# A power of two and its inverse in one masked two-column step of VectorE, and a power of two for z's factor

## The chip, the cores and the metric

One core of a Trainium2 chip runs the kernel. The metric is device microseconds from launch to end of that core, the median of several runs. The kernel before took 486.66 us (three runs, 485.74 to 486.75). TensorE is called PE here, VectorE DVE, ScalarE ACT, GpSimd POOL and SyncE SP, as in the profile.

## The reference

```python
# q, k, v: (8 batches, 8 heads, 576 rows, 64), float32
k_p, v_p = k.reshape(B,H,72,8,D).mean(3), v.reshape(B,H,72,8,D).mean(3)
scores = (q @ k_p.T) / 8;  scores -= scores.max(-1)
attn = exp(scores);  attn /= attn.sum(-1) + 1e-9
x = (attn @ v_p) as (4608 tokens, 512)
h = x @ w_in                                   # (4608, 1024)
e = exp(h - h.max(-1));  sm = e / (e.sum(-1) + 1e-9)
solu = h * sm
ln = (solu - mean(solu)) / sqrt(var(solu) + 1e-6) * g_ln
out = ln @ w_out                               # (4608, 512)
```

q and k are drawn 8 times wider than v. w_in, w_out and g_ln come as float64, so the kernel takes float32 words out of pairs of integers first.

## The kernel before, in words

All matrix products run on PE in float16 with two terms per operand: a high part (the scaled value rounded to float16) and a low part (what the rounding left). To scale without losing bits, q, pooled k, pooled v, w_in, w_out and g_ln each get a power of two just above their largest value, `p`, and its inverse, `s`. `p` comes from a maximum by keeping the exponent bits alone (`exp_bits`, line 276, an integer AND and OR on a 128x1 tile); `s` is its reciprocal in another DVE instruction. For q both are in `q_scale` (line 455: scaled maximum at 461, bits at 467, reciprocal at 472), for k and v in `a_unit` (line 494: bits through line 277, reciprocal at 499), for the weights in `w_bound`, `wi_scale`, `g_all` and `wo_scale` (lines 699 to 766).

The 4608 tokens are 36 tiles of 128. For each tile: q is scaled and split (`q_hi` on ACT, `q_lo` on DVE, line 866), turned, and multiplied with kT into `scores`; DVE and ACT make the softmax (`s_max`, `s_sub`, `s_exp`, `e_sum`, `e_rec`, `e_mul`); POOL makes its low part (`e_lo`, line 978); PE multiplies with v (`av`) and then w_in (`mm1`, tile `hp`). `h_max` and `h_nb` give the bias of the exponential; `z_scale` (line 1056) makes the factor of solu from it in three DVE steps: magnitude of `nb` (1059), reciprocal (1064), minimum with 1 and a per-batch factor (1066). Any factor per row would do, since the normalisation that follows divides it out; `n_u` on POOL puts it into the 1e-6. `z_mul` (line 1073) forms solu, ACT centres and splits it, POOL makes its low part (`z_lo`, line 1093), and `mm2` multiplies with w_out.

The weights are unpacked at the start: DVE joins the words (`w_tail`, line 657), POOL multiplies the sign in (`w_mul`, line 678: 128x1024 in one instruction), and ACT and PE split them. k and v of each later batch are pooled on POOL (line 400).

The order of all this is written out by hand: the table `ORDER` gives every operation a rank, and operations are issued by rank, so each engine runs its own in that order and a late one holds up all that stand behind it on its engine. DMAs and DMA transposes are issued on SP's queue.

Of the kernel before, what the change touches and what calls it, by code (L numbers as in the profile page):

```python
# [10 lines left out]
F32 = mybir.dt.float32  # L11
# [5 lines left out]

EXPMASK = 0x7F800000
S14 = float(2**14)
DEC = 2.0**-111  # L20
# [9 lines left out]
        "a_par.v": (129, 236, 483, 786, 1025, 1171, 1479, 1802),  # L30
        "a_unit.k": (39, 57, 211, 213, 451, 455, 657, 663, 882, 890, 1129, 1155, 1390, 1437, 1615,
        1616),
        "a_unit.v": (131, 134, 254, 261, 500, 503, 804, 805, 1027, 1029, 1180, 1181, 1481, 1482,
        1804, 1805),
        "av": (215, 257, 276, 333, 383, 463, 506, 573, 561, 661, 775, 702, 842, 893, 952, 977,
# [101 lines left out]
        1383, 1444, 1662, 1676, 1722),  # L137
        "q_scale": (30, 31, 32, 183, 189, 190, 231, 232, 247, 436, 443, 446, 666, 670, 671, 718,
        748, 750, 947, 964, 969, 1124, 1127, 1128, 1215, 1216, 1217, 1446, 1447, 1448, 1675, 1677,
        1678, 1723, 1725, 1727),  # L140
        "r_hi": (135, 262, 504, 811, 1085, 1195, 1484, 1806),
# [78 lines left out]
        1883, 1926, 1990, 1980, 2050, 2024),  # L220
        "z_scale": (267, 279, 280, 314, 322, 323, 366, 368, 371, 431, 450, 458, 462, 501, 510,
# [6 lines left out]
        "z_var": (361, 359, 440, 514, 569, 570, 637, 736, 731, 809, 887, 899, 960, 1033, 1104,  # L228
# [6 lines left out]
def kernel(  # L235
# [10 lines left out]
    nc = tc.nc  # L246
# [65 lines left out]
    nc.scalar.activation(ident16, ident, AF.Copy)  # L312
    nc.vector.tensor_scalar(out=identb, in0=ident, scalar1=1.0 / S14, scalar2=None, op0=ALU.mult)
    nc.gpsimd.memset(pmat4, 1.0)
# [13 lines left out]
    nc.gpsimd.memset(phalf, -0.5)  # L328
    for n, c in enumerate((2.0**-11, -(2.0**-11), 2.0**-7)):
        nc.gpsimd.memset(c3[:, n : n + 1], c)  # L330
# [115 lines left out]
    def q_abs(key, part):  # L446
# [6 lines left out]
        )  # L453

    def q_scale(key, n):
        if n == 0:
            st = grp["q", key] = {}
            for x in ("p", "s"):
                st[x] = sm.tile([P, 1], F32, tag=x + "q", name=f"{x}q{key}")
            a = amx["m" if key[0] == "m" else "q"]  # L460
            nc.vector.tensor_scalar(
                out=st["p"], in0=a[:, :1], scalar1=a[:, (1 if key[0] == "b" else 0) :][:, :1],
                scalar2=1.0 / S14, op0=ALU.max, op1=ALU.mult,
            )
# [809 lines left out]
    def group_q(key, t):  # L1274
# [141 lines left out]
    def tile(i):  # L1416
# [56 lines left out]
        op("act", 1.4, t(0, 6.6), h_exp, i, r=[("h", i)] + K("nb") + hk, w=K("z", "se"))  # L1473
        for n in range(2):
            op("dve", 0.2, t(0, 6.7 + 0.2 * n), z_scale, i, n, r=K("nb", "pz") if n else K("nb"),
               w=K("pz"))
        op("dve", 0.21, t(0, 7.3), z_scale, i, 2, r=K("pz") + hk, w=K("rs"))
        op("dve", 1.36, t(0, 7.5), z_mul, i, r=[("h", i)] + K("z", "rs"), w=K("z", "sz"))
# [71 lines left out]
```

## Time and profile before

| | before |
|---|---|
| median of three runs | 486.66 us |
| span of the profiled execution, first to last instruction | 483.6 us |
| PE busy | 456.5 us (94%) |
| DVE busy | 372.2 us (77%), 787 instructions |
| ACT busy | 335.2 us (69%) |
| POOL busy | 304.5 us (63%) |

The profiled execution has no launch around it: its 483.6 us stand against 486.66 us of the median run, so about 3.1 us lie outside the span. The profile lists each instruction's start and length by the source line that made it, what ended a wait before it, and the chain of work that ended last, followed back from the last instruction.

### The profile page before, as it was taken

The numbers are of one execution on the slowest core, as the hardware profiler recorded it, in microseconds if no ns is written. First come the engines' busy times: TensorE is split into PE (matmuls) and PEld (weight loads), VectorE is DVE, ScalarE is ACT, GpSimd is POOL, SyncE is SP. The second block draws the span as 40 slices with busy tenths as digits, with TensorE's granted clock in tenths as the row PEclk, the third lists the DMA queues.
The fourth block names the chain that finished last, engine by engine and source line by source line (L and its number), as shares of the span: only waits on it lengthen the run. The fifth ranks groups of instructions, "written<-read, shape, count | busy, mean of one in ns | idle before, by whom it ended". The sixth has DMA issues, their size and how long they took to land.

```text
span 483.6 us, 14740 instructions
## 1 busy us (share of the span) xinstructions
PE 456.5 (94%) x5976; PEld 287.7 (59%) x5976; DVE 372.2 (77%) x787; ACT 335.2 (69%) x557; POOL 304.5 (63%) x525
## 2 busy tenths in 40 slices
PE   1779899999999999999999999999999999999996
PEld 1655455655655556555556667666776666755553
DVE  5988999999889789878798867678878887462320
ACT  5598887677966688796677657587585697456361
POOL 3459737696697985858953597717758625643532
PEclk9989999999999999999999999999999999999999
DMA  8999389998999899999994999689899576861742
GB/s 309 395 354 225 86 114 219 196 193 138 213 237 213 209 173 207 204 229 229 161 215 111 215 245 172 126 136 243 167 229 190 115 137 117 138 142 24 153 108 69
DMA packets 197749, 88.92 MB, mean 184 GB/s; under 512 B 174121, under 2 KB 182321, under 8 KB 197169
## 3 DMA queue, kind: packets, MB, share of 16 engines
q1 hardware_dynamic: 197680, 87.98, 85.9%
q8 instruction: 47, 0.77, 0.6%
q14 instruction: 22, 0.17, 0.1%
HBM read 36.70 MB, written 9.44 MB: 95 GB/s over the span
## 4 chain that ended last, share of the span: by engine, by line
PE 78%; DVE 16%; DMA 2%; issue 2%; ACT 1%; SPq 0%; POOL 0%; ACTq 0%; DVEq 0%
PE op L274 35%; PE hp L274 31%; PE xp L999 4%; PE sc L274 3%; DMA kr<-in_k_dram 2%; DVE q L866 2%; DVE m L1041 1%; PE krps L410 1%; DVE sc L934 1%; DVE mx L920 1%; DVE sc L923 1%; DVE z L1073 1%; DVE e L949 1%; PE vrps L410 1%; PE res_wi L810 1%
## 5 line engine op out<-in xcount | busy, mean ns | idle before, releaser
L274 PE MATMUL hp<-wi,xT 128*64 128x512 f16 x1728 | 197.2, 379 | 2.8 <-DVE z L1073 1.4
L274 PE MATMUL op<-wo,zT 128*64 128x512 f16 x1728 | 197.2, 379 | 0.1
L274 PEld LDWEIGHTS <-xT 128*64 128x64 f16 x1728 | 106.6, 110 | 75.2 <-ACT xT L1008 2.0
L274 PEld LDWEIGHTS <-zT 128*64 128x64 f16 x1728 | 106.5, 110 | 70.6 <-DMA zT<-z 0.5
L1093 POOL TENSOR_TENSOR z<-z,z 128x512 f16<-128x512 f32 x71 | 82.0, 1167 | 67.9 <-ACT z L1087 66.4
L978 POOL TENSOR_TENSOR e<-e,e 128x512 f16<-128x512 f32 x36 | 42.2, 1173 | 39.7 <-ACT e L972 39.6
L1041 DVE TENSOR_REDUCE m<-hp 128x1 f32<-128x1024 f32 x36 | 43.8, 1217 | 23.1 <-PE hp L274 22.9
L1082 ACT ACTIVATE z<-z,sz 128x1024 f32<-128x1024 f32 x36 | 41.2, 1143 | 17.4 <-DVE z L1073 17.4
L1073 DVE SCALAR_TENSOR_TENSOR z<-hp,rs,z 128x1024 f32<-128x1024 f32 x36 | 46.1, 1280 | 9.1 <-ACT z L1052 7.9
L1052 ACT ACTIVATE z<-hp,nb,Hb 128x1024 f32<-128x1024 f32 x32 | 38.3, 1196 | 11.7 <-DVE nb L1044 9.1
L1151 ACT ACTIVATE osb<-op,f 128x512 f32<-128x512 f32 x36 | 24.5, 679 | 31.3 <-PE op L274 8.1
L1087 ACT ACTIVATE z<-z 128x1024 f16<-128x1024 f32 x36 | 37.7, 1050 | 0.9 <-DMA zT<-z 0.4
L1106 ACT ACTIVATE junk<-z 128x1024 f16<-128x1024 f32 x36 | 37.7, 1048 | 0.3
L400 POOL TENSOR_TENSOR vr<-vr 128x512 f32<-128x512 f32 (+3 forms) x42 | 36.9, 888 | 0.6
L400 POOL TENSOR_TENSOR kr<-kr 128x512 f32<-128x512 f32 (+3 forms) x42 | 36.7, 882 | 1.0 <-DMA kr<-in_k_dram 0.2
L920 DVE TENSOR_REDUCE mx<-sc 128x8 f32<-128x576 f32 x36 | 27.0, 750 | 12.9 <-PE sc L274 12.6
L934 DVE TENSOR_REDUCE sc<-sc 128x8 f32<-128x576 f32 x36 | 27.3, 759 | 12.2 <-ACT sc L930 12.1
L999 PEld LDWEIGHTS <-vb 128*64 128x64 f16 x960 | 28.9, 111 | 6.7 <-DVE vb L574 1.0
L1012 DVE SCALAR_TENSOR_TENSOR xT<-xp,xT 128x512 f16<-128x512 f32 x36 | 24.5, 681 | 8.9 <-ACT xT L1008 8.8
L999 PE MATMUL xp<-eT,vb 128*64 128x128 f16 (+1 forms) x960 | 31.0, 215 | 0.3 <-ACT e L975 0.3
L274 PEld LDWEIGHTS <-qT 128*64 128x64 f16 x1152 | 24.7, 114 | 9.9 <-ACT dg_wi L803 3.4
L1008 ACT ACTIVATE xT<-xp 128x512 f16<-128x512 f32 x36 | 21.2, 589 | 12.2 <-PE xp L999 12.2
(237 smaller groups left out, 621.3 us busy)
## 6 DMA issues: line engine op xcount, KB each, us to landing
kr<-in_k_dram SPq DMA_DIRECT2D x16, 512.0 KB
qr<-in_q_dram SPq DMA_DIRECT2D x16, 512.0 KB
vr<-in_v_dram SPq DMA_DIRECT2D x16, 512.0 KB
out_dram<-osb SPq DMA_DIRECT2D x32, 256.0 KB
wor<-in_moe_w_out_dram SPq DMA_DIRECT2D x4, 1024.0 KB
wo<-in_moe_w_in_dram SPq DMA_DIRECT2D x2, 1024.0 KB
wir<-in_moe_w_in_dram SPq DMA_DIRECT2D x2, 1024.0 KB
zT<-z SPq DMA_TRANSPOSE x72
```

Source lines behind the costliest of these rows:

```text
L274: nc.tensor.matmul(out[lo : lo + 64] if m > 64 else out, lhsT=lhsT[:, lo : lo + 64], **kw)
L400: nc.gpsimd.tensor_tensor(out=dst, in0=src[:, :, :n], in1=src[:, :, n : 2 * n], op=ALU.add)
L934: nc.vector.tensor_reduce(out=tl[i]["r0"], in_=s_view(i), axis=AX.X, op=ALU.add)
L978: nc.gpsimd.tensor_tensor(out=e_main(i, 1), in0=e_src(i)[0], in1=e_main(i, 0), op=ALU.subtract)
L999: nc.tensor.matmul(xp[64 * e : 64 * e + 64, c, lo:hi], lhsT=vb[b % 2][:, n, c, e], rhs=eT[:, 2 * c + e if n < 2 else H + e, lo:hi], start= ...
L1041: nc.vector.tensor_reduce(out=small(i, "m"), in_=tl[i]["hp"], axis=AX.XY, op=ALU.max)
L1052: nc.scalar.activation(z, t["hp"], AF.Exp, bias=t["nb"], scale=hsc(i, 0), accum_out=small(i, "se"))
L1073: nc.vector.scalar_tensor_tensor(out=t["z"], in0=t["hp"], scalar=t["rs"], in1=t["z"], op0=ALU.mult, op1=ALU.mult, accum_out=small(i, "sz"),)
L1082: nc.scalar.activation(t["zf"], t["zf"], AF.Identity, bias=t["sz"], scale=-float(DFF))
L1087: nc.scalar.activation(t["z16"][:, 0], t["zf"], AF.Copy)
L1093: eng.tensor_tensor(out=t["z16"][:, 1, fs], in0=t["zf"][:, fs], in1=t["z16"][:, 0, fs], op=ALU.subtract)
L1106: nc.scalar.activation(junk, t["zf"], AF.Square, scale=DFF**-0.5, accum_out=small(i, "V"))
```

## The change

One helper, `unit`, takes the place of `exp_bits` and the reciprocals. A new constant tile `flip` holds 0 and 2^127 in two columns. One `scalar_tensor_tensor` reads the maximum broadcast to two columns, masks it to the even part of the exponent (`EVENMASK`), and XORs it with `flip`: the first column is then a power of two (at most four times smaller than the maximum's), the second its inverse. The scales around it are moved by the factors 2 and 4 that this leaves. q, k, v, w_in, g_ln and w_out use it. For z, two steps remain of three: the exponent of `nb` is masked and inverted in one integer step, and the minimum follows where the reciprocal stood.

```diff
-    def exp_bits(dst, src):
-        nc.vector.tensor_scalar(
-            out=dst.bitcast(I32), in0=src.bitcast(I32), scalar1=EXPMASK, scalar2=1 << 23,
-            op0=ALU.bitwise_and, op1=ALU.bitwise_or,
+    def unit(dst, src):
+        nc.vector.scalar_tensor_tensor(
+            out=dst.bitcast(I32), in0=src.bitcast(I32).to_broadcast([P, 2]), scalar=EVENMASK,
+            in1=flip.bitcast(I32), op0=ALU.bitwise_and, op1=ALU.bitwise_xor,
         )
...
-    pw1 = const.tile([P, 1], F32, name="pw1")
+    flip = const.tile([P, 2], F32, name="flip")
...
+    for n, c in enumerate((0.0, 2.0**127)):
+        nc.gpsimd.memset(flip[:, n : n + 1], c)
...
+    def pair(key, nm, x):
+        t = sm.tile([P, 2], F32, tag="ps" + nm, name=f"ps{nm}{key}")
+        grp[nm, key].update(p=t[:, :1], s=t[:, 1:])
+        unit(t, x)
...
-        elif n == 1:
-            p = grp["q", key]["p"].bitcast(I32)
-            nc.vector.tensor_scalar(
-                out=p, in0=p, scalar1=EXPMASK, scalar2=1 << 23, op0=ALU.bitwise_and,
-                op1=ALU.bitwise_or,
-            )
-        else:
-            nc.vector.reciprocal(out=grp["q", key]["s"], in_=grp["q", key]["p"])
+        else:
+            pair(key, "q", grp["q", key]["x"])
...
-    def a_unit(nm, key, n):
-        st = grp[nm, key]
-        if n == 0:
-            exp_bits(st["p"], st["p"])
-        else:
-            nc.vector.reciprocal(out=st["s"], in_=st["p"])
+    def a_unit(nm, key):
+        pair(key, nm, grp[nm, key]["x"])
...
+    def w_unit(nm, gm):
+        t = const.tile([P, 2], F32, name=f"ps_{nm}")
+        unit(t, gm)
+        return t[:, :1], t[:, 1:]
...
     def wi_scale():
-        w_bound("wi", 1.0 / S14)
-        sw = const.tile([P, 1], F32, name="sw_wi")
-        nc.vector.reciprocal(out=sw, in_=wst["wi"]["gm"])
-        wst["wi"]["s"] = sw
+        wst["wi"]["p"], wst["wi"]["s"] = w_bound("wi", 2.0 / S14)
...
-        w_bound("wo", 2.0**-13)
+        wst["wo"]["p"], sw = w_bound("wo", 2.0**-11)
         sg = const.tile([P, CO], F32, name="sg_wo")
-        nc.vector.tensor_tensor(
-            out=pw1, in0=wst["wo"]["gm"], in1=wst["gm"], op=ALU.mult
-        )
-        sw = const.tile([P, 1], F32, name="sw_wo")
-        nc.vector.reciprocal(out=sw, in_=pw1)
         nc.vector.tensor_scalar(
-            out=sg, in0=g_sb, scalar1=sw, scalar2=None, op0=ALU.mult
+            out=sg, in0=g_sb, scalar1=sw, scalar2=wst["gs"], op0=ALU.mult, op1=ALU.mult
         )
...
             nc.vector.tensor_scalar(
-                out=small(i, "pz"), in0=t["nb"], scalar1=-1.0, scalar2=t["nb"], op0=ALU.mult,
-                op1=ALU.max,
-            )
-        elif n == 1:
-            nc.vector.reciprocal(out=t["pz"], in_=t["pz"])
+                out=small(i, "pz").bitcast(I32), in0=t["nb"].bitcast(I32), scalar1=EXPMASK,
+                scalar2=EXPMASK, op0=ALU.bitwise_and, op1=ALU.bitwise_xor,
+            )
...
-                out=small(i, "rs"), in0=t["pz"], scalar1=1.0, scalar2=hsc(i, 2), op0=ALU.min,
+                out=small(i, "rs"), in0=t["pz"], scalar1=4.0, scalar2=hsc(i, 2), op0=ALU.min,
...
-        "a_unit.v": (131, 134, 254, 261, 500, 503, 804, 805, 1027, 1029, 1180, 1181, 1481, 1482,
-        1804, 1805),
+        "a_unit.v": (131, 254, 500, 804, 1027, 1180, 1481, 1804),
```

On PE, ACT and SP the order of instructions is the same before and after. POOL has two more memsets at the start. DVE's rows in the program go from 751 to 683. Three places on DVE follow.

The scale of q's first batch, on DVE in the first 21 us. `amx_q` and `amx_k` are the maxima of q and pooled k, `pq`/`sq` the power and its inverse, which are the two columns of `psq` afterwards. Before:

```order
L461 TENSOR_SCALAR pq('b', 0)_205<-amx_q 128x1
L467 TENSOR_SCALAR pq('b', 0)_205<-pq('b', 0)_205 128x1
L472 RECIPROCAL sq('b', 0)_206<-pq('b', 0)_205 128x1
L430 TENSOR_REDUCE amx_k<-kp_87 128x1
L492 TENSOR_REDUCE pk_215<-gk_212 128x1
```

And after:

```order
L462 TENSOR_SCALAR xq('b', 0)_207<-amx_q 128x1
L273 SCALAR_TENSOR_TENSOR psq('b', 0)_209<-xq('b', 0)_207,flip 128x2
L428 TENSOR_REDUCE amx_k<-kp_87 128x1
L486 TENSOR_REDUCE xk_216<-gk_213 128x1
L852 SCALAR_TENSOR_TENSOR q_0_218<-qr_184,psq('b', 0)_209,q_0_218 128x8x64
```

Two instructions with one tensor input each have become one that reads two tensors of SBUF, and the maximum of k stands right behind it.

The scale of w_in, on DVE about 26 us in. `gm_wi` is its bound, `sw_wi` the inverse, `ct` the scale of the scores, `kT` the low part of k that the first scores need. Before:

```order
L499 RECIPROCAL sk_216<-pk_215 128x1
L657 SCALAR_TENSOR_TENSOR wor_288<-wor_288,u_wo_290 128x1024
L690 TENSOR_REDUCE gm_wi<-g_wi 128x1
L701 TENSOR_SCALAR gm_wi<-gm_wi 128x1
L277 TENSOR_SCALAR gm_wi<-gm_wi 128x1
L709 RECIPROCAL sw_wi<-gm_wi 128x1
L561 TENSOR_SCALAR ct('b', 0)_317<-pq('b', 0)_205,pk_215 128x1
L536 SCALAR_TENSOR_TENSOR kT_300<-kTp_230,sk_216,kT_300 128x576
```

And after:

```order
L647 SCALAR_TENSOR_TENSOR wor_289<-wor_289,u_wo_291 128x1024
L680 TENSOR_REDUCE gm_wi<-g_wi 128x1
L691 TENSOR_SCALAR gm_wi<-gm_wi 128x1
L273 SCALAR_TENSOR_TENSOR ps_wi<-gm_wi,flip 128x2
L551 TENSOR_SCALAR ct('b', 0)_316<-psq('b', 0)_209,psk_221 128x1
L526 SCALAR_TENSOR_TENSOR kT_300<-kTp_231,psk_221,kT_300 128x576
```

The reciprocals of k and of w_in are gone, and the new two-input step stands between the join of a w_out word (`wor`), whose end lets POOL multiply its sign, and `kT`.

The factor of z of the first tile, on DVE about 66 us in. Before:

```order
L1044 TENSOR_SCALAR nb_943<-m_891,Hb_860 128x1
L944 RECIPROCAL r_948<-sc_765 128x8
L1059 TENSOR_SCALAR pz_950<-nb_943 128x1
L1012 SCALAR_TENSOR_TENSOR xT_918<-xp_893,xT_918 128x512
L949 TENSOR_TENSOR e_953<-sc_765,r_948 128x576
L866 SCALAR_TENSOR_TENSOR q_5_937<-qr_709,sq('b', 1)_838,q_5_937 128x8x64
L1064 RECIPROCAL pz_950<-pz_950 128x1
L1066 TENSOR_SCALAR rs_994<-pz_950,Hb_860 128x1
L1073 SCALAR_TENSOR_TENSOR z_945,sz_996<-hp_803,rs_994,z_945 128x1024
```

And after:

```order
L1045 TENSOR_SCALAR pz_942<-nb_935 128x1
L998 SCALAR_TENSOR_TENSOR xT_911<-xp_886,xT_911 128x512
L935 TENSOR_TENSOR e_945<-sc_759,r_940 128x576
L852 SCALAR_TENSOR_TENSOR q_5_930<-qr_703,psq('b', 1)_833,q_5_930 128x8x64
L1050 TENSOR_SCALAR rs_985<-pz_942,Hb_854 128x1
L1057 SCALAR_TENSOR_TENSOR z_937,sz_987<-hp_797,rs_985,z_937 128x1024
```

The reciprocal is gone and `rs` stands in its place; both steps left read one tensor.

## Rows read from the trace of the kernel before

**Rows 1.** Stretches: length; busy PE, PEld, DVE, ACT, POOL; granted clock; DMA share, GB/s.

```profile
0.00:120.00 120.00, 96.98 (x1264) 61.94 (x1266) 108.07 (x228) 90.47 (x146) 73.87 (x111) 0.99 0.90 222
120.00:460.00 340.00, 339.95 (x4536) 215.65 (x4534) 261.21 (x553) 235.88 (x399) 223.88 (x398) 1.00 0.89 177
```

**Rows 2.** The chain that ended last, 0 to 125 us: start, us, what.

```profile
26.79 0.74 DVE kT L536
27.67 1.17 PE sc L274 x32
...
115.89 1.22 DVE z L1073 x2
117.15 5.37 PE hp L274 x48
```

**Rows 3.** Waits of PE: what waited for whom, us in total, times, longest.

```profile
PE sc L274 <- DVE kT L536: 3.2, 1, 3.2
```

**Rows 4.** Timeline of DVE, 18 to 27 us: start, length, instruction.

```profile
18.95 0.15 DVE L467 TENSOR_SCALAR pq('b', 0)_205<-pq('b', 0)_205 128x1 int32<-128x1 int32 x1
19.36 0.49 DVE L430 TENSOR_REDUCE amx_k<-kp 128x1 bf16<-128x320 f32 x1
...
24.56 0.16 DVE L499 RECIPROCAL sk<-pk 128x1 f32<-128x1 f32 x1
...
26.33 0.15 DVE L277 TENSOR_SCALAR gm_wi<-gm_wi 128x1 int32<-128x1 int32 x1
26.52 0.16 DVE L709 RECIPROCAL sw_wi<-gm_wi 128x1 f32<-128x1 f32 x1
26.60 0.20 DVE L561 TENSOR_SCALAR ct('b', 0)_317<-pq('b', 0)_205,pk 128x1 f32<-128x1 f32 x1
26.71 0.81 DVE L536 SCALAR_TENSOR_TENSOR kT<-kTp,sk,kT 128x576 f16<-128x576 f32 x1
```

**Rows 5.** Timeline of POOL, 17 to 31 us.

```profile
17.92 2.12 POOL L678 TENSOR_TENSOR wo<-wo,sg_wi 128x1024 f32<-128x1024 f32 x1
26.04 2.14 POOL L678 TENSOR_TENSOR wor<-wor,sg_wo 128x1024 f32<-128x1024 f32 x1 [6.00 <-DVE wor L657]
28.14 2.16 POOL L678 TENSOR_TENSOR wir<-wir,sg_wi 128x1024 f32<-128x1024 f32 x1
```

**Rows 6.** Timeline of DVE, two instructions that read two SBUF tensors.

```profile
46.61 2.17 DVE L866 SCALAR_TENSOR_TENSOR q<-qr,sq('b', 0)_206,q 128x512 f16<-128x512 f32 x1
...
177.47 0.74 DVE L591 SCALAR_TENSOR_TENSOR vr<-vp,sv,vr 64x64 f16<-64x64 f32 x1
```

**Rows 7.** Timeline of POOL at the same places.

```profile
45.80 1.19 POOL L400 TENSOR_TENSOR kp<-kr 128x128 f32<-128x128 f32 x3
46.95 2.43 POOL L400 TENSOR_TENSOR vr<-vr 128x512 f32<-128x512 f32 x2
...
176.98 1.16 POOL L978 TENSOR_TENSOR e<-e,e 128x512 f16<-128x512 f32 x1
```

**Rows 8.** Lines 591 and 866 alone: ns of one, least/median/most, first and last start.

```profile
L591 DVE SCALAR_TENSOR_TENSOR vr<-vp,sv,vr x8: 271/278/970, 45.7 to 395.5; 64x64 f16<-64x64 f32 x8
L866 DVE SCALAR_TENSOR_TENSOR q<-qr,sq('b', 1)_838,q x4: 741/742/752, 67.6 to 88.3; 128x512 f16<-128x512 f32 x4
```

**Rows 9.** Groups of DVE instructions by shape: busy us, mean ns of one, idle before.

```profile
L760 DVE TENSOR_TENSOR pw<-gm_wo,gm_g 128x1 f32<-128x1 f32 x1 | 0.2, 159 | 0.0
```

**Rows 10.** Timeline of DVE, 64 to 104 us: the bits of v's and k's power.

```profile
64.58 0.15 DVE L277 TENSOR_SCALAR pv<-pv 128x1 int32<-128x1 int32 x1
...
103.38 0.15 DVE L277 TENSOR_SCALAR pk<-pk 128x1 int32<-128x1 int32 x1
```

**Rows 11.** Timeline of POOL at the same places.

```profile
63.93 2.13 POOL L678 TENSOR_TENSOR wor<-wor,sg_wo 128x1024 f32<-128x1024 f32 x1 [3.45 <-ACT sg_wo L675]
...
102.67 1.16 POOL L978 TENSOR_TENSOR e<-e,e 128x512 f16<-128x512 f32 x1
```

**Rows 12.** A stretch, PE alone: length, busy, granted clock, DMA share, GB/s.

```profile
27.00:30.50 3.50, 2.83 (x42) 0.52 1.05 404
```

More of the change, by code (lines that the diff above doesn't have):

```diff
@@ L18 @@
 EXPMASK = 0x7F800000
+EVENMASK = 0x7F000000
 S14 = float(2**14)
@@ L30 @@
         "a_par.v": (129, 236, 483, 786, 1025, 1171, 1479, 1802),
-        "a_unit.k": (39, 57, 211, 213, 451, 455, 657, 663, 882, 890, 1129, 1155, 1390, 1437, 1615,
-        1616),
-        "a_unit.v": (131, 134, 254, 261, 500, 503, 804, 805, 1027, 1029, 1180, 1181, 1481, 1482,
-        1804, 1805),
+        "a_unit.k": (39, 211, 451, 657, 882, 1129, 1390, 1615),
+        "a_unit.v": (131, 254, 500, 804, 1027, 1180, 1481, 1804),
         "av": (215, 257, 276, 333, 383, 463, 506, 573, 561, 661, 775, 702, 842, 893, 952, 977,
@@ L137 @@
         1383, 1444, 1662, 1676, 1722),
-        "q_scale": (30, 31, 32, 183, 189, 190, 231, 232, 247, 436, 443, 446, 666, 670, 671, 718,
-        748, 750, 947, 964, 969, 1124, 1127, 1128, 1215, 1216, 1217, 1446, 1447, 1448, 1675, 1677,
-        1678, 1723, 1725, 1727),
+        "q_scale": (30, 31, 183, 189, 231, 232, 436, 443, 666, 670, 718, 748, 947, 964, 1124,
+        1127, 1215, 1216, 1446, 1447, 1675, 1677, 1723, 1725),
         "r_hi": (135, 262, 504, 811, 1085, 1195, 1484, 1806),
@@ L220 @@
         1883, 1926, 1990, 1980, 2050, 2024),
-        "z_scale": (267, 279, 280, 314, 322, 323, 366, 368, 371, 431, 450, 458, 462, 501, 510,
[6 rows of a table removed]
+        "z_scale": (267, 279, 314, 322, 366, 368, 431, 450, 462, 501, 527, 529, 588, 610, 624,
[4 rows of a table added]
         "z_var": (361, 359, 440, 514, 569, 570, 637, 736, 731, 809, 887, 899, 960, 1033, 1104,
@@ L312 @@
     nc.scalar.activation(ident16, ident, AF.Copy)
-    nc.vector.tensor_scalar(out=identb, in0=ident, scalar1=1.0 / S14, scalar2=None, op0=ALU.mult)
+    nc.vector.tensor_scalar(out=identb, in0=ident, scalar1=2.0 / S14, scalar2=None, op0=ALU.mult)
     nc.gpsimd.memset(pmat4, 1.0)
@@ L328 @@
     nc.gpsimd.memset(phalf, -0.5)
-    for n, c in enumerate((2.0**-11, -(2.0**-11), 2.0**-7)):
+    for n, c in enumerate((0.0, 2.0**127)):
+        nc.gpsimd.memset(flip[:, n : n + 1], c)
+    for n, c in enumerate((2.0**-11, -(2.0**-11), 2.0**-9)):
         nc.gpsimd.memset(c3[:, n : n + 1], c)
@@ L453, in q_abs @@
         )
+    def pair(key, nm, x):
+        t = sm.tile([P, 2], F32, tag="ps" + nm, name=f"ps{nm}{key}")
+        grp[nm, key].update(p=t[:, :1], s=t[:, 1:])
+        unit(t, x)
     def q_scale(key, n):
         if n == 0:
-            st = grp["q", key] = {}
-            for x in ("p", "s"):
-                st[x] = sm.tile([P, 1], F32, tag=x + "q", name=f"{x}q{key}")
+            st = grp["q", key] = {"x": sm.tile([P, 1], F32, tag="xq", name=f"xq{key}")}
             a = amx["m" if key[0] == "m" else "q"]
             nc.vector.tensor_scalar(
-                out=st["p"], in0=a[:, :1], scalar1=a[:, (1 if key[0] == "b" else 0) :][:, :1],
-                scalar2=1.0 / S14, op0=ALU.max, op1=ALU.mult,
-            )
-        elif n == 1:
-            p = grp["q", key]["p"].bitcast(I32)
-            nc.vector.tensor_scalar(
-                out=p, in0=p, scalar1=EXPMASK, scalar2=1 << 23, op0=ALU.bitwise_and,
-                op1=ALU.bitwise_or,
+                out=st["x"], in0=a[:, :1], scalar1=a[:, (1 if key[0] == "b" else 0) :][:, :1],
+                scalar2=2.0 / S14, op0=ALU.max, op1=ALU.mult,
             )
         else:
-            nc.vector.reciprocal(out=grp["q", key]["s"], in_=grp["q", key]["p"])
+            pair(key, "q", grp["q", key]["x"])
     def spread(src, n, name):
@@ L489, in a_all @@
         st = grp[nm, key]
-        for x in ("p", "s"):
-            st[x] = sm.tile([P, 1], F32, tag=x + nm, name=f"{x}{nm}{key}")
-        nc.vector.tensor_reduce(out=st["p"], in_=st["g"], axis=AX.XY, op=ALU.max)
-    def a_unit(nm, key, n):
-        st = grp[nm, key]
-        if n == 0:
-            exp_bits(st["p"], st["p"])
-        else:
-            nc.vector.reciprocal(out=st["s"], in_=st["p"])
+        st["x"] = sm.tile([P, 1], F32, tag="x" + nm, name=f"x{nm}{key}")
+        nc.vector.tensor_reduce(out=st["x"], in_=st["g"], axis=AX.XY, op=ALU.max)
+    def a_unit(nm, key):
+        pair(key, nm, grp[nm, key]["x"])
     def k_tile(b):
@@ L703, in w_bound @@
         )
-        exp_bits(gm, gm)
+        return w_unit(nm, gm)
+    def w_unit(nm, gm):
+        t = const.tile([P, 2], F32, name=f"ps_{nm}")
+        unit(t, gm)
+        return t[:, :1], t[:, 1:]
     def wi_scale():
-        w_bound("wi", 1.0 / S14)
-        sw = const.tile([P, 1], F32, name="sw_wi")
-        nc.vector.reciprocal(out=sw, in_=wst["wi"]["gm"])
-        wst["wi"]["s"] = sw
+        wst["wi"]["p"], wst["wi"]["s"] = w_bound("wi", 2.0 / S14)
     def w_pwi():
         nc.gpsimd.tensor_scalar(
-            out=pw3, in0=c3, scalar1=wst["wi"]["gm"], scalar2=None, op0=ALU.mult
+            out=pw3, in0=c3, scalar1=wst["wi"]["p"], scalar2=None, op0=ALU.mult
         )
@@ L771, in w_pwo @@
         nc.gpsimd.tensor_scalar(
-            out=pwo, in0=pw1, scalar1=-(2.0**-8), scalar2=None, op0=ALU.mult
+            out=pwo, in0=wst["wo"]["p"], scalar1=wst["gp"], scalar2=-(2.0**-8), op0=ALU.mult,
+            op1=ALU.mult,
         )
@@ L1113, in n_u @@
         nc.gpsimd.tensor_scalar(
-            out=u, in0=t["pz"], scalar1=1.0, scalar2=None, op0=ALU.min
+            out=u, in0=t["pz"], scalar1=4.0, scalar2=0.25, op0=ALU.min, op1=ALU.mult
         )
@@ L1212, in scale @@
                 w=[("p" + nm, key), ("s" + nm, key)])
-        for j in range(2):
-            n_ = op("dve", 0.16, t + 0.7 + 0.2 * j, a_unit, nm, key, j, u=[("p" + nm, key)],
-                    w=[("s" + nm, key)], after=[n_])
+        op("dve", 0.16, t + 0.7, a_unit, nm, key, u=[("p" + nm, key)], w=[("s" + nm, key)],
+           after=[n_])
     def pool(b, nm, t):
@@ L1283, in group_q @@
         prev = None
-        for j in range(3):
+        for j in range(2):
             prev = op("dve", 0.18, t + 2.2 + 0.2 * j, q_scale, key, j,
-                      r=[] if j else [("am", "q", key)], u=[("sq", key)] if j == 2 else [],
-                      w=[("pq", key), ("sq", key)] if j < 2 else [("sq", key)], after=[prev])
+                      r=[] if j else [("am", "q", key)], w=[("pq", key), ("sq", key)],
+                      after=[prev])
             if j == 0:
@@ L1473, in tile @@
         op("act", 1.4, t(0, 6.6), h_exp, i, r=[("h", i)] + K("nb") + hk, w=K("z", "se"))
[L1474 to L1477, printed above, removed]
+        op("dve", 0.2, t(0, 6.7), z_scale, i, 0, r=K("nb"), w=K("pz"))
+        op("dve", 0.21, t(0, 7.3), z_scale, i, 1, r=K("pz") + hk, w=K("rs"))
         op("dve", 1.36, t(0, 7.5), z_mul, i, r=[("h", i)] + K("z", "rs"), w=K("z", "sz"))
```

4 lines of the change are left out of this document (1 added, 3 removed), and 10 rows, old and new, of the table ORDER.

## The prediction, made before the changed kernel ran

> **What bounds the kernel now.** I read the stretches first, then the chain of waits, then the waits of PE, then the timelines of DVE and POOL side by side. The stretches split the kernel in two [rows 1]: from 120 to 460 us PE is busy for 339.95 of 340.00 us, so nothing that DVE saves there can shorten it; before 120 us PE is busy for 96.98 us and DVE for 108.07. Whatever the change is worth is decided in the first 120 us, by when PE gets its work. The chain shows the hand-over [rows 2]: `z_mul` of a tile ends at 117.11 us, PE goes on at 117.15 us, and from there it is PE to the end. Its first step on this side of the loads is `kT` at 26.79, then the first scores at 27.67 us, for which PE had stood 3.2 us [rows 3]. In between PE and DVE pass the delay to and fro, so a step of DVE that comes later there makes the end later, and one that comes earlier makes it earlier.
>
> **The change part by part.** It removes one instruction of DVE for each power of two (q, k, v, w_in, g_ln), two for w_out and one per tile for z. A removed step is worth between 0.08 us, where the next is independent (26.52 to 26.60), and 0.19 us, where it sits in a chain (26.33 to 26.52) [rows 4]. The z step that stays reads one tensor as before: 0.
>
> What it adds is a new kind of instruction: the step that makes both numbers reads two tensors in SBUF. Its own length is not in the trace; the nearest rows are 159 ns for a two-input step of one column [rows 9] and 278 ns for one of 64 columns [rows 8]. I take 0.16 us, the same as what it replaces.
>
> The cost is elsewhere. Two-input steps of DVE are stretched when POOL is in the middle of an instruction. The one of 64 columns took 0.74 us at 177.47 [rows 6] instead of 0.28 [rows 8], beside a POOL instruction from 176.98 to 178.14 [rows 7]: it must have begun at 177.93, 0.2 us before POOL's row ended. The q step at 46.61 took 2.17 us instead of 0.74, so it began at 48.04, about 0.2 us before the first of two POOL instructions of 1.2 us from 46.95 ended [rows 6 to 8]. So I price a unit step that meets a running POOL instruction as: it starts when that row ends, less 0.2 us, and all of DVE behind it waits.
>
> [...]
>
> Now the places, in the times of before.
> - q's first batch. The unit step is due at 18.95; POOL multiplies signs from 17.92 to 20.04 [rows 4, 5]. It starts at 19.84, and `amx_k`, which stood at 19.36, follows at about 19.95: +0.6 us. Behind it wait PE's spread of k's maximum and the whole of DVE's queue.
> - w_in. Without k's reciprocal at 24.56 DVE is 0.1 us better, so +0.5. POOL's next sign instruction (26.04 to 28.18) is released by DVE itself [rows 5], so it moves to 26.54 to 28.68. The unit step comes to 26.83 and is let in at 28.48. `ct` and `kT` follow in 0.24 us: `kT` starts at 28.72 instead of 26.71, +2.0 us, and the first scores with it.
> - From 28 to 48 us everything behind moves by these 2.0 us, POOL's work too, since it hangs on the same softmax. The unit steps of g, v and w_out lie here, and two removed steps of w_out; but the q step at 46.61 waits 1.43 us for POOL in any case [rows 6, 7], so what is lost here up to that, and all that is gained, is swallowed: 0.
> - From 48 to 117 us twelve steps go: five of z, three of q, two of k, two of v. At 0.08 to 0.19 us that is 1.0 to 2.3 us; most stand between independent steps, so I take 0.1 each: -1.2 us.
> - v of the second batch. The step due at 64.58 meets the last sign instruction (63.93 to 66.06) [rows 10, 11]; it starts at 65.86: +1.3 us.
> - k of the third batch. Due at 103.38 within 102.67 to 103.83 [rows 10, 11]: it starts at 103.63, +0.25 us. The other unit steps between 48 and 117 us I put at 0.
>
> The sum is 2.0 + 0 - 1.2 + 1.3 + 0.25 = +2.35 us. The profiled span of 483.6 us becomes 486.0 us; the median of the runs lies 3.1 us above the span, so 486.66 becomes 489.0 us. After 120 us the waits come too, but PE has no gap there that they could open at once.
>
> [...]
>
> **The rivals.**
> 1. Faster: the new step is not held up. It reads two columns only, and no row of before shows a two-input step in the middle of a sign instruction of 2.1 us. Then `amx_k` gains nothing (it waits for pooled k), `kT` gains 0.1 for k's reciprocal and 0.19 for w_in's, 28 to 48 us is swallowed, and 1.2 us come after: -1.5 us, 485.2 us. Against it stands the 64-column step [rows 6 to 8], whose own work is hardly longer. It decides if the unit step of w_in is under 0.3 us long in the new trace. [...]
> 2. A missed turn: POOL's sign instructions stand back to back (28.14 starts before 26.04 + 2.14 ends [rows 5]). The q step at 46.61 was not let in where POOL's short ones changed over at 46.99 [rows 6, 7]. If w_in's step misses the change at 28.18, it waits for 2.1 us more: 491.1 us. For it that row, against it that long instructions let DVE in at 48.04.
> 3. No change: the 2.0 us vanish in PE's later stops. PE is idle for 23 us of the first 120 [rows 1], some of it after 28 us. Then only the later terms count, +0.35 us: 487.0 us. Against it: those stops are waits for DVE, which is held up itself.
>
> **How the numbers follow.** The forecast has 0.60, rival 1 0.13, rival 2 0.14, rival 3 0.13. The forecast's own range is 487.7 to 490.3 us: a removed step at 0.19 instead of 0.1 gives 1.1 us back, a missed small turn or a longer unit step of 0.28 us (eleven of them, 0.12 each) costs up to 1.3. The range to hold eight in ten reaches down to 486.0 and up to 491.4 us; below lies most of rival 1. A change of 0.2%, 1.0 us, is what can be told from none here. Faster by more: most of rival 1, 0.11. Within: rival 3 and the rest, 0.16. Slower: 0.73.
>
> **What would show it.** In the new profile, the unit steps (line 273) should be of two kinds: 0.16 us where POOL is idle, and 0.9 us for q's first batch, 1.6 us for w_in, 1.3 us for v's second batch, each ending with a POOL instruction of the sign line. PE's wait for `kT` should be about 5.2 us. If all unit steps are short, rival 1 is right; if PE's wait is longer but PE stands busy from before 120 us as now, rival 3; if w_in's step is near 3.7 us, rival 2. I am wrong altogether if the time moves through anything after 120 us.

## The result: slower by more than twice the forecast

The changed kernel took 492.75 us (median of five runs, 491.19 to 494.73) against 486.75 us of the kernel before (485.74 to 487.06). The ratio is 1.0121, interval 1.0099 to 1.0143: 6.0 us slower where 2.3 us were forecast, and outside the range. The execution whose profile is shown was the longest of the five (494.73 us, span 493.0; the other four spans are 489.5 to 491.5), so a difference between the two traces can be larger than that of the medians: the profiled spans, 493.0 and 483.6 us, are 9.4 us apart.

The stretches answer [rows 1] and [rows 12]; the columns are the same.

```profile
0.00:120.00 120.00, 94.65 (x1164) 60.35 (x1166) 105.86 (x196) 86.61 (x136) 71.74 (x105) 0.94 0.86 214
120.00:460.00 340.00, 337.31 (x4550) 224.31 (x4548) 258.90 (x512) 237.15 (x404) 224.26 (x396) 1.00 0.87 175
25.30:35.30 10.00, 5.51 (x46) 2.72 (x46) 8.51 (x12) 7.88 (x9) 5.28 (x4) 0.50 0.98 307
49.10:52.40 3.30, 3.30 (x23) 1.35 (x23) 3.17 (x7) 2.40 (x5) 3.21 (x6) 0.50 0.15 50
```

DVE is busy 2.2 us less before 120 us, but PE too, by 2.3 us: what DVE saves, PE doesn't get. After 120 us PE now stands for 2.7 of 340 us, where it stood for 0.05. The granted clock was 0.50 in two stretches, of 10 and 3.3 us; before, it was 0.52 in one of 3.5.

The waits of PE (whom it waited for, us in all, times, longest). The first was 3.2 us before [rows 3], the second 0.8.

```profile
PE sc L270 <- DVE kT L526: 4.7, 1, 4.7
PE g_wo L270 <- DVE g_wo L676: 2.6, 1, 2.6
...
PE gv L270 <- DVE amx_v L428: 1.4, 2, 1.0
```

The chain that ended last, to 125 us, answers [rows 2]. Four unit steps (line 273) now stand on it.

```profile
18.74 1.20 DVE psq('b', 0)_209 L273
...
26.94 1.85 DVE ps_wi L273
28.91 0.73 DVE kT L526
29.79 1.17 PE sc L270 x32
...
45.23 2.14 DVE psv L273
...
68.75 1.41 DVE psv L273
```

The first scores start at 29.79 instead of 27.67 us. Here are DVE, then POOL, around the first two held steps; they answer [rows 4] and [rows 5].

```profile
18.74 1.20 DVE L273 SCALAR_TENSOR_TENSOR psq('b', 0)_209<-xq('b', 0)_207,flip 128x2 int32<-128x2 int32 x1
19.94 0.49 DVE L428 TENSOR_REDUCE amx_k<-kp 128x1 bf16<-128x320 f32 x1
...
21.64 0.15 DVE L273 SCALAR_TENSOR_TENSOR psk<-xk,flip 128x2 int32<-128x2 int32 x1
...
26.94 1.85 DVE L273 SCALAR_TENSOR_TENSOR ps_wi<-gm_wi,flip 128x2 int32<-128x2 int32 x1
28.72 0.20 DVE L551 TENSOR_SCALAR ct('b', 0)_316<-psq('b', 0)_209,psk 128x1 f32<-128x1 f32 x1
28.84 0.80 DVE L526 SCALAR_TENSOR_TENSOR kT<-kTp,psk,kT 128x576 f16<-128x576 f32 x1
```

```profile
17.80 2.12 POOL L668 TENSOR_TENSOR wo<-wo,sg_wi 128x1024 f32<-128x1024 f32 x1
26.66 2.12 POOL L668 TENSOR_TENSOR wor<-wor,sg_wo 128x1024 f32<-128x1024 f32 x1 [6.73 <-DVE wor L647]
28.73 2.14 POOL L668 TENSOR_TENSOR wir<-wir,sg_wi 128x1024 f32<-128x1024 f32 x1
```

With POOL idle the step takes 0.15 us (21.64). The one at 18.74 ends at 19.94, POOL's product at 19.92; the one at 26.94 ends at 28.79, POOL's at 28.78. That is the mechanism and the size of the forecast. Next, DVE and then POOL at v of the first batch and the q step of [rows 6] and [rows 7].

```profile
45.23 2.14 DVE L273 SCALAR_TENSOR_TENSOR psv<-xv,flip 128x2 int32<-128x2 int32 x1
47.29 0.41 DVE L676 TENSOR_REDUCE g_wo<-bnd_wo 128x1 f32<-128x256 f32 x1
...
52.30 0.74 DVE L852 SCALAR_TENSOR_TENSOR q<-qr,psq('b', 0)_209,q 128x512 f16<-128x512 f32 x1
```

```profile
44.00 2.13 POOL L668 TENSOR_TENSOR wor<-wor,sg_wo 128x1024 f32<-128x1024 f32 x1
46.09 3.16 POOL L398 TENSOR_TENSOR kr<-kr 128x512 f32<-128x512 f32 x4
49.22 1.14 POOL L398 TENSOR_TENSOR kp<-kr 128x128 f32<-128x128 f32 x3
50.31 2.07 POOL L398 TENSOR_TENSOR vr<-vr 128x512 f32<-128x512 f32 x2
```

The step of v came at 45.23, wasn't let in where POOL changed over at 46.1, and ended only at 47.37, among the four sums that followed. The maximum of w_out's bound (`g_wo`) stood behind it, and PE waited for that. The q step that took 2.17 us before takes 0.74 here: moved by 5.7 us, it comes just as one of POOL's sums ends (52.38). So there was nothing to swallow the loss.

Here are DVE and POOL at v of the second batch, answering [rows 10] and [rows 11].

```profile
68.66 1.50 DVE L273 SCALAR_TENSOR_TENSOR psv<-xv,flip 128x2 int32<-128x2 int32 x1
```

```profile
68.01 2.13 POOL L668 TENSOR_TENSOR wor<-wor,sg_wo 128x1024 f32<-128x1024 f32 x1 [2.28 <-ACT sg_wo L665]
```

It ends at 70.16, POOL's product at 70.14. Last, DVE, POOL and PE around 250 us, where before PE had no gap.

```profile
249.92 0.66 DVE L273 SCALAR_TENSOR_TENSOR psq('m', 2)_4611<-xq('m', 2)_4604,flip 128x2 int32<-128x2 int32 x1
250.50 2.13 DVE L273 SCALAR_TENSOR_TENSOR psk<-xk,flip 128x2 int32<-128x2 int32 x1
252.56 1.21 DVE L1027 TENSOR_REDUCE m<-hp 128x1 f32<-128x1024 f32 x1
```

```profile
250.48 0.30 POOL L967 TENSOR_TENSOR e<-e,e 128x64 f16<-128x64 f32 x1
250.74 0.45 POOL L398 TENSOR_TENSOR vp<-vr 128x128 f32<-128x128 f32 x1
251.15 1.15 POOL L964 TENSOR_TENSOR e<-e,e 128x512 f16<-128x512 f32 x1
252.27 0.30 POOL L967 TENSOR_TENSOR e<-e,e 128x64 f16<-128x64 f32 x1
```

```profile
259.29 0.25 PE L270 MATMUL gv<-identb,amx_v 128*64 128x128 bf16 x2 [0.99 <-DVE amx_v L428]
...
260.53 0.86 PE L985 MATMUL xp<-eT,vb 128*64 128x128 f16 x24 [0.47 <-DVE pz L1045]
```

Two unit steps one after the other hold DVE up for 2.7 us, through changes of POOL at 250.74, 251.15 and 252.27. The row maximum (line 1027) and all behind it are late, and the batch's next maximum, `amx_v`, misses PE by 0.99 us. In the trace of before that maximum ended at 249.51 us and PE took it up at 250.54, so the margin, 1.0 us, could be read there:

```profile
249.02 0.49 DVE L430 TENSOR_REDUCE amx_v<-vp 128x1 bf16<-128x320 f32 x1
250.54 0.22 PE L274 MATMUL gv<-identb,amx_v 128*64 128x128 bf16 x2
```

### The profile page after: what moved, and what is told of

Read it like the earlier page. It is cut to its first block, busy times and chain, and to the rows that moved or that the text cites. A ratio compares the mean times of both kernels' runs of the same rounds, so it can differ in the third digit from the quotient of the medians.

```text
span 493.0 us, 14666 instructions
## 1 busy us (share of the span) xinstructions
PE 461.0 (94%) x5976; PEld 303.2 (62%) x5976; DVE 371.3 (75%) x719; ACT 336.1 (68%) x557; POOL 306.5 (62%) x527
## 4 chain that ended last, share of the span: by engine, by line
PE 76%; DVE 14%; DMA 6%; issue 2%; ACT 2%; SPq 1%; POOL 0%; ACTq 0%; DVEq 0%
PE op L270 33%; PE hp L270 29%; PE xp L985 4%; PE sc L270 3%; DMA qr<-in_q_dram 3%; PE res_wi L796 2%; DMA eT<-e 2%; DMA qT<-q 1%; DVE q L852 1%; DVE z L1057 1%; PE vrps L408 1%; DVE m L1027 1%; DVE mx L906 1%; DVE psv L273 1%; DVE amx_q L440 1%
## 5 line engine op out<-in xcount | busy, mean ns | idle before, releaser
L270 PEld LDWEIGHTS <-xT 128*64 128x64 f16 x1728 | 112.5, 110 | 67.7 <-ACT xT L994 1.5
L270 PEld LDWEIGHTS <-zT 128*64 128x64 f16 x1728 | 114.2, 110 | 64.3 <-DMA zT<-z 1.2
L270 PE MATMUL sc<-kT,qT 128*64 128x72 f16 x1152 | 26.1, 200 | 5.8 <-DVE kT L526 4.7
```

What stands on the lines that cost most here:

```text
L270: nc.tensor.matmul(out[lo : lo + 64] if m > 64 else out, lhsT=lhsT[:, lo : lo + 64], **kw)
```

## The experiments

Each ratio is to the kernel before, run on the same chip beside it.

**Two one-input steps.** The changed kernel, with the unit step cut in two:

```diff
-        nc.vector.scalar_tensor_tensor(
-            out=dst.bitcast(I32), in0=src.bitcast(I32).to_broadcast([P, 2]), scalar=EVENMASK,
-            in1=flip.bitcast(I32), op0=ALU.bitwise_and, op1=ALU.bitwise_xor,
-        )
+        for n in range(2):
+            nc.vector.tensor_scalar(
+                out=dst[:, n : n + 1].bitcast(I32), in0=src.bitcast(I32), scalar1=EVENMASK,
+                scalar2=n * EVENMASK, op0=ALU.bitwise_and, op1=ALU.bitwise_xor,
+            )
```

> The changed kernel, but the power and its inverse come from two steps of one tensor input each (mask; mask and XOR) in place of the one step that reads two tensors of SBUF. The z part and the order stay. Blocked reads (the two-input step waits for POOL): no step of line 273 and 274 is over 0.3 us, PE's wait for kT is 3.0 us or less, and the time is 485.2 us, 0.3% under before. Shifted order (the steps that are gone move other work of DVE and SP into worse places): the time stays near that of the changed kernel, 491 to 493 us, since the order is the same. Clock alone: as blocked reads, since without the longer stop of PE its clock does not fall longer.

Measured: 483.36 us, ratio 0.993 (0.9913 to 0.9947), faster than both kernels, and 1.8 us under what I expected. The two steps of w_in, beside the same POOL product (26.38 to 28.52):

```profile
26.67 0.21 DVE L274 TENSOR_SCALAR ps_wi<-gm_wi 128x1 int32<-128x1 int32 x2
26.80 0.20 DVE L552 TENSOR_SCALAR ct('b', 0)_319<-psq('b', 0)_209,psk 128x1 f32<-128x1 f32 x1
26.92 0.81 DVE L527 SCALAR_TENSOR_TENSOR kT<-kTp,psk,kT 128x576 f16<-128x576 f32 x1
```

Together they take 0.21 us instead of 1.85. The new arithmetic is harmless; the form of the step is not.

**The two halves of the change.** z's part alone on the kernel before (its `z_scale` of two steps, and the factor 4 that goes with it), and the unit steps alone (z's three steps put back):

> The kernel before with the z part of the change alone (two z steps of three). Blocked reads: both z steps read one tensor, so nothing waits; up to five reciprocals of 0.1 to 0.19 us are gone before PE is saturated, 0 to 0.7 us faster: 486.0 to 486.7 us. Shifted order: slower by a good part of the 6 us, since 36 of the 68 steps that are gone are these.

> The changed kernel with the three z steps of before. Blocked reads: all of the loss stays, 492 to 494 us. Shifted order: about half of it or less, 487 to 490 us.

Measured: z alone 485.41 us, 0.9968 (0.9956 to 0.9981); unit steps alone 494.43 us, 1.0155 (1.0142 to 1.0168). z's part is a gain of 1.6 us, more than the 0 to 0.7 us expected: PE's wait for z, 1.4 us in the trace of before, is 0.4 us in this one. The unit steps carry all of the loss.

**The step by itself.** A bench: on DVE small steps, each behind a reduction of 0.68 us, beside rows of POOL products of 2.34 us.

> Not the kernel: a small program that leaves the whole computation out and writes zeros. DVE runs four kinds of small step, each behind a reduction of 128x512: one SBUF input (line 61), two SBUF inputs (line 67, the step of the change), one SBUF and one PSUM input (line 73), a product of two SBUF tensors (line 79); first with POOL idle, then beside POOL's products of 128x1024, then beside POOL's memsets of 128x1024. Blocked reads: with POOL idle all take 0.15 to 0.2 us; beside the products lines 67 and 79 take 1 us in the mean and up to 2 us or, where a turn is missed, 4 us, lines 61 and 73 stay at 0.15 to 0.25 us; beside the memsets all stay short. If the step itself is slow (integer form, broadcast input), line 67 is long with POOL idle as well and line 73 too.

DVE groups beside the products (the last column is idle time):

```profile
L67 DVE SCALAR_TENSOR_TENSOR dst<-src,flip 128x2 int32<-128x2 int32 x12 | 20.9, 1743 | 0.1
...
L61 DVE TENSOR_SCALAR dst<-src 128x1 int32<-128x1 int32 x15 | 2.2, 148 | 0.2
L73 DVE SCALAR_TENSOR_TENSOR dst<-src,flip_p 128x2 int32<-128x2 int32 x8 | 1.2, 145 | 0.0
```

The unit step takes 1743 ns on average here (2.27 us at most), and 150 ns where POOL stands. With the second input in PSUM (`flip_p`), the same integer form and the same broadcast, it takes 145 ns: these are not the cause. A product of two float tensors of SBUF (line 79) is held as well, 1638 ns. Beside POOL memsets, which read nothing, a product of two tensors of SBUF took 161 ns. Step and reduction together are one POOL product long (both come every 2.30 us): here each product let one step in at its end.

**One held step at a time.** The kernel with two one-input steps, with the two-input step back at chosen places:

```diff
-    def unit(dst, src):
...
+    def unit(dst, src, key):
+        if key in BOTH:
...
+            return
+        for n in range(2):
...
```

`BOTH` is q's first batch and w_in; v of the first batch; the batches scaled after 95 us; v of the second batch.

> The version with one-input steps (483.4 us), with the two-input step put back for q's first batch and w_in alone, the two places ahead of the first scores. Delay of kT with the clock: kT is 2.0 us later, PE stands about 4.7 us, the granted clock stays at its lower level for longer and PE's next work starts 3.4 us later, as in the changed kernel; all of it reaches the end: 486.5 to 487 us. Swallowed: the delay vanishes in waits before 120 us, 483.4 to 484.5 us.

> The version with one-input steps, with the two-input step put back for v's first batch alone. If it meets POOL's sign instruction near 42 us: up to 2 us longer, PE's wait for w_out's bound grows by as much and the end moves by 1 to 2 us: 484.5 to 485.5 us. If it is swallowed by the q step near 47 us, as the prediction had it: 483.4 us.

> The version with one-input steps, with the two-input step put back for all batches whose scale is made after 95 us (k and v from the third on, q's 2 to 7, the mixed groups 1 to 3). If PE has no gap that they open (the prediction): 483.4 us. If DVE's stalls of up to 2.1 us reach PE there too, as the gaps of the changed kernel after 120 us suggest (2.7 us in its trace): 484.5 to 486.5 us.

> The kernel with two one-input steps, with the two-input step back for v of the second batch alone. Theory (each of these steps is held to the end of POOL's instruction, and what PE then loses stays): this one is 1.5 us long, the time 484.2 to 485.2 us, that is 0.8 to 1.8 us above the 483.4 us of the kernel with none. Rival (a stop at 65 us is swallowed by the stops that PE has before 120 us anyway): under 0.5 us above it, 483.0 to 483.9 us.

| two-input step at | us | ratio (interval) | lengths of the steps, us |
|---|---|---|---|
| q's first batch and w_in | 485.99 | 0.9979 (0.9966 to 0.9991) | 1.12, 1.85 |
| v of the first batch | 485.86 | 0.9972 (0.9957 to 0.9987) | 2.14 |
| all after 95 us | 485.75 | 0.9979 (0.9963 to 0.9995) | 0.15 to 2.78 |
| v of the second batch | 485.77 | 0.9959 (0.9943 to 0.9975) | 1.50 |

The first three ran on one chip with a kernel of the next experiment that holds no step (0.9937). Against it they lose 0.0042, 0.0035 and 0.0042 of 487.19 us, or 2.0, 1.7 and 2.0 us (1.6, 1.5 and 1.4 us by the medians), and no interval touches its interval. But that kernel also has the added matmuls, and its clock doesn't fall (1.00 from 25 to 60 us); and the kernel with two one-input steps, without them, gave 0.993 and 0.9954 (below) on two other chips. So it is shown that these steps cost time, but their sizes are good to about 1 us only. v of the second batch lies 0.0029 above the one of these and 0.0005 above the other; that it costs anything at the end is not shown. With v of the first batch held, PE's wait for `g_wo` is 2.6 us; with two one-input steps it is 0.7. With the late steps PE's gap of the changed kernel is back:

```profile
251.93 0.25 PE L271 MATMUL gv<-identb,amx_v 128*64 128x128 bf16 x2 [1.20 <-DVE amx_v L436]
...
253.17 0.86 PE L993 MATMUL xp<-eT,vb 128*64 128x128 f16 x24 [0.47 <-DVE pz L1053]
```

It is there in all five profiled kernels with the step at this place (0.99 to 1.34 us), and in none without it.

**The clock.** Matmuls whose results nobody reads, between w_in's bound and the first scores: 12 in the kernel with two one-input steps, 18 in the changed one.

```diff
+        if nm == "wi":
+            for _ in range(18):
+                nc.tensor.matmul(
+                    wst[nm]["bnd"], lhsT=ident16,
+                    rhs=sel.rearrange("p h t j r -> p (h t j r)")[:, :512], start=True, stop=True,
+                )
```

> The version with one-input steps, and 12 matmuls of 128x512 more on PE behind w_in's bound, whose results nobody reads, in the stop before the first scores. If the clock's fall from 27.7 to 31.1 us costs what its work says (3.4 us at half clock, some 1.1 to 1.7 us of work) and that work is on the path: the fall is gone and the time is 482.0 to 482.5 us. If it is not on the path: 483.4 us; if the matmuls come in the way of the first scores: over 484 us.

> The changed kernel with 18 more matmuls on PE between w_in's bound and the first scores, whose results nobody reads: they keep PE at work while it would stand, so that its clock does not fall at the first scores. If the longer fall of the clock (10.2 us of 0.5 against 3.4 before) is a part of the 6 us, as it was 1.3 us at the pooled v's product: the time falls by 1 to 1.5 us, to 491.0 to 491.8. If it is swallowed by the held-up step of v's first batch that follows, as it was swallowed in the kernel without two-input steps: 492.3 to 493.2 us.

Measured: 484.39 us, 0.9937 (0.9923 to 0.9951), in the first, no gain over 0.993; 491.5 us, 1.0095 (1.0077 to 1.0113), in the second, 1.3 us under 1.0121. In the first the matmuls are not in the way: from `g_wi` to the first scores PE takes 3.5 us with them (25.04 to 28.53) as without (24.38 to 27.87). The changed kernel so kept busy, in the stretch of its first fall and in another:

```profile
25.30:35.30 10.00, 9.24 (x81) 5.33 (x80) 8.93 (x13) 9.03 (x11) 5.59 (x4) 1.00 1.04 322
46.10:49.40 3.30, 3.23 (x8) 1.58 (x9) 3.10 (x10) 2.13 (x6) 3.30 (x7) 0.50 0.05 20
```

The first fall, of 10 us, is gone (1.00 instead of 0.50); the second, of 3.3 us, is still there (0.50) and only comes 3 us earlier. PE's stop for `g_wo` is 3.4 us long instead of 2.6, so a part of what the clock gave back went into waiting for DVE. The first fall is worth 1.3 us in the changed kernel (the intervals overlap, so this isn't secured), and nothing that can be measured where the first stop is short.

**One instruction, the maximum as a scalar.** `flip` as the only tensor, the maximum as a scalar per partition:

```diff
+        nc.vector.tensor_scalar(
+            out=dst.bitcast(I32), in0=flip.bitcast(I32), scalar1=src.bitcast(I32),
+            scalar2=EVENMASK, op0=ALU.bitwise_xor, op1=ALU.bitwise_and,
         )
```

> The changed kernel with one edit: the unit step stays one instruction, but reads the two columns of flip as its only tensor input and the maximum as a scalar per partition (XOR first, then the mask; the same numbers come out). As many DVE instructions as the changed kernel. Theory (the price is that of two tensors of SBUF read in one step beside POOL): every unit step is about 0.15 us long, PE waits about 3.1 us for kT as with two one-input steps, and the time is that of the kernel with two one-input steps or up to 0.5 us under it, 482.5 to 484.0 us. Rival (the price is that of a step with a second operand from SBUF of any kind, or of the order with fewer steps): unit steps of 1 to 2 us stay, and the time is 491 to 494 us.

Measured: 493.46 us, 1.014 (1.0119 to 1.0161), and w_in's step is as long as ever:

```profile
27.21 1.85 DVE L273 TENSOR_SCALAR ps_wi<-flip,gm_wi 128x2 int32<-128x2 int32 x1
```

My theory of this run fell: "two tensors of SBUF" is too narrow a name for what is held. So the forms were benched.

> The computation is left out; six forms of small steps stand on DVE, each behind a reduction of 0.6 us, eight of each beside a row of POOL products of 2.3 us. What held the step with the scalar per partition (1.16 and 1.85 us where 0.22 was seen alone)? Theory A, the number of columns: a step with one column goes through whatever its scalar is (the scale ct, 128x1 with a scalar from SBUF, took 0.20 us beside a POOL product in the kernel before), a step that reads two columns of one tensor of SBUF and writes two is held even with constants. So one column with constants and one column with a scalar under 0.3 us, two columns with constants and two with a scalar about 1.7 us on average. Theory B, the second operand from SBUF: one and two columns with a scalar about 1.7 us, one and two columns with constants under 0.3 us. By both the step of two tensors with one column is held, 1.7 us, unless two columns were what held that one too (then under 0.3 us). [...]

DVE groups beside POOL products:

```profile
L76 DVE TENSOR_SCALAR dst<-flip,src 128x2 int32<-128x2 int32 x8 | 14.3, 1791 | 0.0
L82 DVE SCALAR_TENSOR_TENSOR dst<-src,flip 128x1 int32<-128x1 int32 x8 | 14.2, 1781 | 0.0
L70 DVE TENSOR_SCALAR dst<-flip 128x2 int32<-128x2 int32 x8 | 13.3, 1668 | 0.0
L64 DVE TENSOR_SCALAR dst<-flip,src 128x1 int32<-128x1 int32 x8 | 1.6, 204 | 0.0
L58 DVE TENSOR_SCALAR dst<-src 128x1 int32<-128x1 int32 x3 | 0.4, 144 | 0.0
```

Theory A holds: two columns of one tensor are held with constants alone (1668 ns), one column isn't, whatever its scalar (144 ns with constants, 204 with a scalar). Two tensors are held even with one column (1781 ns). The twelve steps of the sixth form (line 88: six columns, read 2 by 3 and written 3 by 2) all ran before the POOL products began, so this bench says nothing on it; the expectation below takes its 211 ns for more than it is.

**One instruction that isn't held.** The changed kernel's count and order of steps, with six columns:

```diff
+        nc.vector.tensor_scalar(
+            out=dst.rearrange("p (a b) -> p a b", b=3)[:, :, :2].bitcast(I32),
+            in0=flip.rearrange("p (b a) -> p b a", b=2)[:, :, :3].bitcast(I32),
+            scalar1=src.bitcast(I32), scalar2=EVENMASK, op0=ALU.bitwise_xor, op1=ALU.bitwise_and,
         )
```

> The changed kernel, its count and order of steps kept; the unit step reads six columns of one constant (two groups of three) and writes them as three groups of two, with the maximum as the scalar per partition; its first two outputs are the power and the inverse. Alone beside POOL products this form took 211 ns where the two-column form took 1267 ns on average. Theory (the 6 us are the steps held behind POOL and what follows from them, nothing else of the change costs): every unit step is 0.2 to 0.3 us, PE waits 3.0 to 3.3 us for kT, and the time is that of two one-input steps or a little less, 482.8 to 484.3 us. Rival (fewer steps or their order cost by themselves, and two one-input steps hid it by the earlier first scale): the steps are as short, and the time stays above 485.5 us.

Measured: 485.57 us (482.64 to 487.32), 0.996 (0.9938 to 0.9982). All unit steps took 0.20 to 0.22 us, w_in's in the middle of a product (26.20 to 28.34):

```profile
26.49 0.22 DVE L273 TENSOR_SCALAR ps_wi<-flip,gm_wi 128x6 int32<-128x6 int32 x1
```

Why this form goes through beside POOL, while two columns of one tensor with a scalar are held (1791 ns in the bench, 1.85 us at w_in), no run shows. The loss is gone, but the time lies above what I expected (482.8 to 484.3 us) and just above 485.5, where I had set the rival, that fewer steps or their order cost something by themselves. Both kernels without a held step therefore ran once more, on one chip:

> The kernel with two one-input steps once more, beside the one with the six-column step on the same chip. If the 0.3% between the two (0.993 against 0.996 in runs at different times) is a property of the kernels: this one 483.0 to 484.0 us, 1.5 to 2.5 us under the six-column kernel. If it is scatter between chips and times: the two medians within 1 us of each other.

> The kernel with the six-column step once more. If its 68 steps fewer, or their order, cost something against two one-input steps: 485 to 486 us and 1.5 to 2.5 us above the other kernel of this call. If scatter: within 1 us of it, 483.5 to 485.5 us.

Measured: 484.39 us, 0.9954 (0.9932 to 0.9976), and 485.33 us, 0.997 (0.995 to 0.999). The medians are 0.94 us apart, within the 1 us I had set for scatter. But six columns were slower both times (0.996 and 0.997 against 0.993 and 0.9954), so whether two one-input steps are better by about 1 us stays open. Against the loss of the changed kernel this is small: the rival is no explanation of it.

## Why the prediction was wrong

The direction is right, and so are the mechanism and the lengths of the steps at q's first batch, w_in and v of the second batch. Three costs that count for nothing in its sum are not nothing: v of the first batch, the steps after 120 us and, probably, the granted clock.

- *Unit steps wait for POOL's row to end, less 0.2 us.* Right at q's first batch (let in at 19.79, row's end 19.92), w_in (28.64, 28.78) and v of the second batch (70.01, 70.14): 0.13 us before the end, not 0.2. Wrong at v of the first batch and at k around 250 us, which missed one and three changes of POOL. That the hold makes the loss is shown by other forms of the same step: two that POOL doesn't hold give 0.993 to 0.997, two that it holds 1.0121 and 1.014.
- *q's first batch and w_in, +2.0.* Right: the first scores come 2.1 us later, and 2.0 us of the end go when these two alone are held. PE's stop is 4.7 us and not the 5.2 forecast, since it begins 0.6 us later (`g_wi` on PE at 24.67 instead of 24.04).
- *28 to 48 us: swallowed, 0.* Wrong. v of the first batch lost 2.14 us by missing POOL's change at 46.1, which I had as rival 2, but for w_in. The cover I named, the q step at 46.61, was no cover: its own wait was a matter of when it came, and it came later. Alone this step costs 1.7 us.
- *48 to 117 us: -1.2 for twelve steps fewer.* The whole change without the hold gains 1.5 to 3.4 us. The price of 0.1 us a step was too low for z: its five steps come to 0.5 us by it, and z's part alone gained 1.6.
- *v of the second batch, +1.3.* 1.50 us long as against 0.15; that it costs anything at the end isn't shown.
- *k of the third batch, +0.25.* 0.55 us long at 107.89; it is one of the late steps and was not tried alone.
- *After 120 us no gap that they could open.* Wrong. No gap in the trace of before is no margin: `amx_v` came to PE in time by 1.0 us, and two steps of DVE lost 2.4 us at 250 us (2.7 less the 0.3 that they take alone). The late steps alone cost 2.0 us.
- *The granted clock, no term of the sum.* Probably 1.3 us, by the changed kernel kept busy (1.0095 against 1.0121). Around the stop of 4.7 us the clock was 0.50 for 10 us, where it was 0.52 for 3.5 us around the stop of 3.2 us before, and it was 0.50 again for 3.3 us from 49.1 us, after the stop of 2.6 us for `g_wo`.

The three costs are 1.7, 2.0 and up to 1.3 us (some of the last is in the 2.0 of the first two steps), against 3.7 us that were missing. With sizes good to about 1 us this shows that they are enough, not that they add up exactly: v, k, g and w_out of the other places were not tried one by one.

Of the rivals, 1 is what happens without the hold (forecast 485.2 us; measured 483.4 to 485.6), 2 happened at another step, 3 did not happen.

## What to carry to other kernels

Before two small DVE steps are merged into one, look at what the merged one reads beside POOL: a step of 0.15 us became one of up to 2.1 us, and everything behind it in DVE's order was late (`kT` started at 28.84 instead of 26.71 us). Two one-column steps with constants did the same work here 8 to 9 us faster than one two-input step (483.4 to 484.4 against 492.75 us), and with z's part the kernel so made beat the kernel before by 0.5 to 0.7%. And a cost may be put at nothing only for a cover that doesn't move itself: a wait that depends on when a step comes, or an engine that is busy without a known margin, covers nothing. The margin can be read: when the producer ended, and when the busy engine took up its result.

## What the runs showed that I had not expected

- A step of one tensor with constants, 128x2 in and out, is held by POOL as two tensors are: 1668 ns instead of 158 ns (two tensors with one column: 1781 instead of 148). With 128x1 it isn't (144 ns), nor with six columns written 3 by 2 and read 2 by 3 (0.22 us).
- A held step can miss a change of POOL: 2.14 us at 45.23, 2.13 us at 250.50 and up to 2.78 us among the late ones, though it stood waiting at the change. In the bench one was let in at the end of each product. What decides this stays open.
- How long the granted clock stays near 0.5 [rows 12] does not follow from the length of PE's stop alone. Around a stop of 4.6 to 4.7 us before the first scores it was about 10 us in all four profiles (25.3 to 35.3 us: 0.50 in the changed kernel, 0.51 with q's first batch and w_in held). Around one of 2.9 to 3.3 us it was about 3.4 us in five profiles (before, z's part alone, two one-input steps twice, v of the first batch; 0.52 from 27 to 30.5 us in the first of these, 0.50 from 27.67 to 31.09 with two one-input steps) and about 6.7 us in four: both with six columns, the late steps, and v of the second batch (the mean from 0 to 120 us is 0.97 with six columns, 0.99 with two one-input steps). The last two run the same steps up to 60 us as the kernel with two one-input steps, so it can differ between executions of the same work: the executions of the kernel before alone have means from 0.991 to 0.996.
